# Fused attention and feed-forward on one core: unit loads, place and engine of the weight conversion's steps, one round more

## The chip, the core and the metric

The kernel runs on one core of a Trainium2 chip. The metric is the device time in microseconds of one execution; the median of three runs of the kernel before is 602.66 us (602.04 to 603.43). Engines are called by their names and, in the profile, by short ones: TensorE (PE; PEld is its weight load), VectorE (DVE), ScalarE (ACT), GpSimd (POOL), SyncE (SP, which here only issues transfers).

## What is computed

A decayed linear attention over blocks of 64 positions, then two feed-forward layers. The weights of the layers arrive as float64.

```python
def _attn_ref(q, k, v, lam):                 # B, H, S, D = 2, 8, 768, 64
    for b in range(S // 64):
        intra = (qb @ kb.T * Dmask) @ vb                 # Dmask = lam ** (i - j), i >= j
        inter = (qb * lam_pow) @ kv_state
        out[:, :, sl] = intra + inter
        kv_state = lam_block * kv_state + (kb * rev_pow).T @ vb
def _moe_ref(x, w_in, w_out):                # 1536 x 512, d_ff 2048
    h = x @ w_in
    g = where(h >= 1, h, where(h <= -1, 0, (h + 1) ** 2 / 4))
    return g @ w_out
def _moe2_ref(x, w_gate, w_val, w_out):      # d_ff 1536
    return (sigmoid(x @ w_gate) * (x @ w_val)) @ w_out
```

## The kernel before

**Attention.** It is cut into 16 units (batch, pair of heads, half of the sequence) and runs in 8 pairs of units, `for k in range(nu // 2)`; blocks of 128 positions are used. A unit's data is one array of 128 rows with four parts of 384 values: q, k, k by rows, v by rows. For each unit `scores` (L825) multiplies q and k on TensorE, `weigh` (L854) multiplies by the decay table `DT` on VectorE into `pT`, `values` (L886) multiplies with v; `pre_k` (L793, L800) scales k into `kd`, `updates` (L843) makes the state's increments, `states` (L869) scans them on VectorE, `pre_q` (L811) scales q on GpSimd into `qs`, `queries` (L905) adds the part from the state. `high` (L917, ScalarE) and `low` (L921, VectorE) split the result into `xh` and `xl`, two parts whose products stand for one product of higher precision.

**Loads.** `u_load` loads a unit through SP. Units 0 to 3 come in two transfers each (L694, rows of 3 KB), units 4 and 5 in four each (L686, rows of 1.5 KB), the later ones in one (L699, rows of 6 KB). In `tables` the first halves of units 0, 1 and 2 go first, then their second halves, units 3 and 4, then the tables `qp` and `DT`, which come through a DRAM buffer `pd` in rows of 512 bytes, then unit 5 and the others. `scores` of units 0, 1 and 2 stand ahead of the pairs.

**Conversion of the weights.** A piece is 128x512 float64 values, in the order `pieces`; pieces 0 to 3 are the first layer's input weights for its first four groups of columns n, 4 to 7 the output weights of the same groups. SP loads it into one of three `raw` tiles. Then *words* (`w_words`: two passes on ScalarE, L107 and L109, or three behind the attention, L107, L114, L115), *float* (`w_float`: L121 and L123 on VectorE, then an integer addition L125), *high* (`w_high`, L129 on ScalarE, the rounded half) and *low* (`w_low`, L133, the rest). Behind the attention a round (`w_round`) does one such step for each of three successive pieces, addition and rest on VectorE. In the attention the steps are jobs, W for words, F for float, H for high and low: the table `JOBS` gives for a pair a list for each of three places, and there the addition and the rest are on GpSimd. The places are: behind the scan, behind the weighing, and at the pair's end.

**Feed-forward in the attention's tail.** `feed_forward` is a generator whose steps are drawn by `next(steps)` in pairs 5 to 7. `hidden(n)` (L227, L228, L229) is 12 matmuls for group n and a block of 512 tokens: the high half of the piece first, the low half second. u0, u1, ... below are the entries of `seq`, u0 to u3 being n = 0 to 3 of the first tokens. Behind each, ScalarE (L259, L254) and VectorE (L263, *r*) make the activation, ScalarE (L246, *gh*) and VectorE (L247, *gl*) split it. `project` (L282) multiplies with the output weights (pieces 4 to 7) into four banks `a`; `flush` (L300, L302) copies them into `part`. In pair 5 hidden(0) is drawn, in pair 6 hidden(1) and hidden(2), in pair 7 hidden(3). When the attention is over, `finish` does a projection and a round. `forms_first` adds sums of `xh` and `xl` (*f*, L384) on VectorE between these.

On each engine instructions run in the order in which the program writes them (`tc.manual_schedule()`); between engines only the semaphores of shared tiles order them.

```python
if k - 1 in AFT: next(steps)     # behind states(k)
convert()                        # first place
...
for i in ahead: weigh(i)
convert()                        # second place
queries(a); queries(b); high(a); low(a)
...
if k in AFT: next(steps)
convert()                        # third place
```

Of the kernel before, what the change touches and what calls it, by code (L numbers as in the profile page):

```python
# [7 lines left out]
F32 = mybir.dt.float32  # L8
# [10 lines left out]
P = 128  # L19
NP = H // 2  # L20
CU = 3
UT = CU * P
NHALF = S // UT
TT = 512
# [5 lines left out]
CST = 4 + PADW + P  # L30
NS = 2 * CU - 1
FORE, AFT = (6, 7), (5, 6)
JOBS = {4: (("W0",), ("F0",), ()), 5: (("H0", "W1"), ("F1",), ("H1", "W2")),
        6: (("F2", "H2"), ("W3",), ("F3", "W4")), 7: (("H3", "F4"), ("W5", "H4"), ("F5", "W6"))}
NQD = 2
UB = 6
NEARLY, NWIDE = 6, 4
WARM = 2
NWP, NRAW = 10, 3

# [2 lines left out]
def fused_kernel(ctx: ExitStack, tc: tile.TileContext, qkv, qd, cst, w1, w2, out):  # L43
# [150 lines left out]
    def w_job(job):  # L194

        i = int(job[1:])
        if job[0] == "W":
            assert prog["round"] == i and prog["loaded"] > i
            prog["round"] += 1
            w_words(i)  # L200
            w_load()
        elif job[0] == "F":
            w_float(i, pool)
        else:
            w_high(i)
            w_low(i, pool)
            w_forms(i)
# [27 lines left out]
    seq = []  # L235
# [96 lines left out]
    def feed_forward():  # L332
        def finish():
            project(*behind.pop(0))
            if u is not seq[-1]:
                w_round()

        for u in seq:
            n, t, first, last = u
            h = hidden(n, t, 0)  # L340
            split()
            yield
            r = act1(h, n, t)
            act1_end(r, h)
            fresh.append((u, r))
            yield
            j = seq.index(u)
            while attention_over and len(behind) >= (4 if j < NEARLY else 3 if j < 8 else 2):
                finish()
        split()  # L350
# [312 lines left out]
    with ExitStack() as actx:  # L663
# [11 lines left out]
        raw_u = {}  # L675

        def u_load(i, js=range(2)):
# [1 line left out]
                return  # L679
            b, p, h = units[i]  # L680
            if NWIDE <= i < NEARLY:
                tag = ("gh", "gl")[i - NWIDE]
                raw_u[i] = [gp.tile([P, TT], F32, tag=tag, name=f"u{i}_{j}")[:, 0:UT]
                            for j in range(4)]
                for j in range(4):
                    sp.dma_start(out=raw_u[i][j], in_=qkv[b, p, h][:, j])  # L686
                return
            if i < NEARLY:

# [32 lines left out]
        def tables():  # L722
# [2 lines left out]
            dm = [tp.tile([P, 512], F32, tag="r", bufs=5, name=f"dm{j}")[:, 0:2 * (PADW + P)]  # L725
                  .rearrange("p (h x) -> p h x", h=2) for j in range(2)]
            sp.dma_start(out=cs[:, 0:CST], in_=cst)
            for j in range(2):
                for i in range(3):
                    u_load(i, (j,))  # L730
            for i in range(3, 5):
                u_load(i)
            dve.memset(zero, 0.0)
            for j in range(2):
# [51 lines left out]
        def pre_k(i):  # L786
# [1 line left out]
            b, p, h = units[i]  # L788
            kd[i] = sp2.tile([P, CU, 2, D], F32, tag="kd", name=f"kd{i}")
            for e in range(2):  # L790
                if i < 1 and not e or i // 2 - 1 in AFT and e:

                    pool.tensor_tensor(  # L793
                        out=kd[i][:, :, e],
                        in0=raw_u[i][2].rearrange("p (c h d) -> p c h d", c=CU, h=2)[:, :, e],
                        in1=DT[:, 2 * p + e, P - 1:P].unsqueeze(1).to_broadcast([P, CU, D]),
                        op=ALU.mult,
                    )
                    continue
# [124 lines left out]
        with tc.manual_schedule():  # L924
            tables()
            warm()
            for i in range(3):
                scores(i)
            pre_k(0)
            pre_k(1)  # L930
# [5 lines left out]
            for k in range(nu // 2):  # L936
                a, b = 2 * k, 2 * k + 1
                ahead = [i for i in (a + 2, b + 2) if i < nu]
                jobs = iter(JOBS.get(k, ((), (), ())))

                def convert():
                    for job in next(jobs):
                        w_job(job)

                if k:
# [14 lines left out]
                convert()  # L960
                for i in ahead:
                    pre_k(i)
                    if i != 2:
                        scores(i)
                if k == 0:
                    weigh(1)
                if k in FORE:
# [5 lines left out]
                queries(b)  # L973
                high(a)
                low(a)
                if ahead:
                    decay(k + 1)
                for i in ahead:
# [96 lines left out]
```

## Time and profile before

| | |
|---|---|
| median of three runs | 602.66 us |
| profiled execution, its own time | 602.4 us |
| its span | 600.6 us |
| TensorE busy | 582.8 us, 97% |
| VectorE busy | 439.8 us, 73% |
| ScalarE busy | 373.9 us, 62% |
| GpSimd busy | 86.9 us, 14% |
| granted clock, mean | 0.994 |

A profile is one execution. Spans and timelines count from its first instruction; its own time is 1.8 us longer than the span. Matmuls overlap in the pipeline, so a busy TensorE need not be at its peak: the distance from start to start tells the pace. The timeline gives behind an instruction the idle time of its engine ahead of it and what ended that time. Idle time on an engine that nothing waits for costs nothing. The page's 40 slices show loads at 291 to 375 GB/s in the first three slices (15 us each) and little later, and the granted clock at full in all slices but the fifth.

### The profile page before, as it was taken

What the parts mean: (1) busy time and instruction counts of PE and PEld (TensorE: products, weight loads), DVE (VectorE), ACT (ScalarE), POOL (GpSimd) and SP (SyncE); (2) the same over time, 40 slices, a digit from 0 to 9 for tenths busy, and PEclk for the clock granted to TensorE, in tenths of its full rate; (3) what the DMA queues carried; (4) which work ended last, traced back from release to release, by engine and by line L of the source; (5) the groups of instructions that cost most, each with busy time, mean ns of one, the idle gap of its engine ahead of it and who ended that gap; (6) DMA issues with size and microseconds to landing.
All of it is one profiled execution on the core that took longest, in us unless ns stands there. A gap on an engine that the chain in (4) does not pass through costs nothing.

```text
span 600.6 us, 8055 instructions
## 1 busy us (share of the span) xinstructions
PE 582.8 (97%) x3060; PEld 480.4 (80%) x3060; DVE 439.8 (73%) x717; ACT 373.9 (62%) x661; POOL 86.9 (14%) x92
## 2 busy tenths in 40 slices
PE   7898789999999999999999999999999999999997
PEld 5787568888888888888888887888888888888886
DVE  7685578879797978888788997694684685584444
ACT  6457576689686868676786687673583583451220
POOL 4446400000000000000000001231141151060000
PEclk9999799999999999999999999999999999999999
DMA  8991232012121221212131233131132031000013
GB/s 291 375 367 69 79 136 102 2 70 94 48 73 68 72 70 69 72 44 75 59 105 47 80 109 106 46 113 64 35 106 70 24 113 41 2 0 1 0 71 140
DMA packets 16678, 52.59 MB, mean 88 GB/s; under 512 B 1784, under 2 KB 4096, under 8 KB 16640
## 3 DMA queue, kind: packets, MB, share of 16 engines
q1 hardware_dynamic: 16624, 52.08, 25.3%
q8 instruction: 24, 0.39, 0.3%
q14 instruction: 14, 0.11, 0.1%
q10 hardware_dynamic: 16, 0.01, 0.0%
HBM read 48.92 MB, written 3.15 MB: 87 GB/s over the span
## 4 chain that ended last, share of the span: by engine, by line
PE 85%; DVE 5%; ACT 4%; DMA 3%; POOL 2%; issue 1%; SPq 0%; POOLq 0%; DVEq 0%; ACTq 0%
PE a L282 35%; PE p L418 25%; PE h L228 7%; PE h L229 7%; PE h L227 7%; DMA u<-in_qkv 3%; PE x L905 1%; PE x L886 1%; PE s L825 1%; DVE part L409 1%; POOL wr L125 1%; POOL w L133 1%; ACT xth L370 0%; ACT w L129 0%; DVE wr L125 0%
## 5 line engine op out<-in xcount | busy, mean ns | idle before, releaser
L282 PE MATMUL a<-gh,w 128*128 128x512 f32 x384 | 118.7, 390 | 2.0 <-DVE w L133 2.0
L304 DVE TENSOR_TENSOR part<-part,a 128x512 f32<-128x512 f32 x132 | 83.3, 680 | 12.4 <-PE a L282 12.4
L227 PE MATMUL h<-xh,w 128*128 128x512 f32 x224 | 88.3, 394 | 3.3 <-ACT w L129 3.3
L228 PE MATMUL h<-xh,w 128*128 128x512 f32 x224 | 88.5, 395 | 1.9 <-POOL w L133 1.9
L282 PE MATMUL a<-w,gh 128*128 128x512 f32 x288 | 88.7, 389 | 0.0
L229 PE MATMUL h<-xl,w 128*128 128x512 f32 x224 | 88.1, 393 | 0.0
L282 PEld LDWEIGHTS a<-gh,w 128*128 128x128 f32 x384 | 72.0, 188 | 17.6 <-DVE w L133 2.4
L282 PE MATMUL a<-gl,w 128*128 128x512 f32 x192 | 74.7, 389 | 0.0
L282 PEld LDWEIGHTS a<-w,gh 128*128 128x128 f32 x288 | 54.1, 188 | 11.2
L151 POOL TENSOR_TENSOR wr<-wr 128x256 f32<-128x256 f32 x16 | 13.2, 824 | 328.7 <-DVE w L133 328.1
L282 PE MATMUL a<-w,gl 128*128 128x512 f32 x144 | 56.0, 389 | 0.0
L129 ACT ACTIVATE w<-wr 128x512 fp32r<-128x512 f32 x68 | 42.4, 623 | 21.1 <-POOL wr L125 11.2
L227 PEld LDWEIGHTS h<-xh,w 128*128 128x128 f32 x224 | 42.5, 190 | 12.7 <-ACT w L129 3.6
L228 PEld LDWEIGHTS h<-xh,w 128*128 128x128 f32 x224 | 42.6, 190 | 11.4 <-POOL w L133 2.7
L229 PEld LDWEIGHTS h<-xl,w 128*128 128x128 f32 x224 | 42.6, 190 | 8.8
L133 DVE TENSOR_TENSOR w<-wr,w 128x512 fp32r<-128x512 f32 x63 | 47.0, 746 | 3.2 <-ACT w L129 3.2
L114 ACT ACTIVATE wc<-raw 128x512 uint16<-128x512 uint32 x61 | 47.9, 785 | 0.0
L107 ACT ACTIVATE wr<-raw 128x512 f32<-128x512 f32 x68 | 45.1, 663 | 4.2 <-POOL s L159 3.6
L115 ACT ACTIVATE wc<-raw 128x512 f16<-128x512 f32 x61 | 47.0, 770 | 0.0
L125 DVE CUSTOM_DVE_ANT_0 wr<-wr,wc 128x1024 uint16<-128x1024 uint16 x62 | 44.0, 709 | 3.0 <-ACT wc L115 0.2
L246 ACT ACTIVATE gh<-r 128x512 fp32r<-128x512 f32 x40 | 25.0, 625 | 30.4 <-DVE r L263 20.1
L282 PEld LDWEIGHTS a<-gl,w 128*128 128x128 f32 x192 | 36.0, 188 | 7.4
(117 smaller groups left out, 1048.2 us busy)
## 6 DMA issues: line engine op xcount, KB each, us to landing
raw<-in_w SPq DMA_DIRECT2D x68, 512.0 KB, 3.4
u<-in_qkv SPq DMA_DIRECT2D x10, 768.0 KB, 8.8
u<-in_qkv SPq DMA_DIRECT2D x8, 384.0 KB, 6.4
out<-part SPq DMA_DIRECT2D x12, 256.0 KB, 2.1
u<-in_qkv SPq DMA_DIRECT2D x8, 192.0 KB, 5.6
DT<-pd SPq DMA_DIRECT2D x1, 256.0 KB, 5.7
qp<-pd SPq DMA_DIRECT2D x2, 96.0 KB, 4.9
DT<-pd SPq DMA_DIRECT2D x1, 128.0 KB, 5.8
```

Source lines behind the costliest of these rows:

```text
L107: act.activation(r, hi.bitcast(F32), AF.Copy, scale=2.0 ** -112)
L114: act.activation(limb(U16)[:, :, 0], lo, AF.Copy, scale=2.0 ** -29)
L115: act.activation(limb(F16)[:, :, 1], hi.bitcast(F32), AF.Copy, scale=2.0 ** -60)
L125: eng.tensor_tensor(out=ri, in0=ri, in1=c, op=ALU.add)
L129: act.activation(ws[i][:, 0], tmps[i][0], AF.Copy)
L133: eng.tensor_tensor(out=ws[i][:, 1], in0=r, in1=ws[i][:, 0].bitcast(F32), op=ALU.subtract)
L227: pe.matmul(h, lhsT=wh, rhs=xh[:, k, tt], start=(k == 0), stop=False)
L228: pe.matmul(h, lhsT=wl, rhs=xh[:, k, tt], start=False, stop=False)
L229: pe.matmul(h, lhsT=wh, rhs=xl[:, k, tt], start=False, stop=(k == NP - 1))
L282: pe.matmul(accs[j], lhsT=a, rhs=b_, start=(first and m == 0), stop=(last and m == 2))
L304: dve.tensor_tensor(out=o, in0=o, in1=accs[j], op=ALU.add)
L418: pe.matmul(o, lhsT=a, rhs=b_, start=(start and k == 0 and m == 0), stop=(k == HK - 1 and m == 2), skip_group_check=True)
```

## The change

Loads: units 0 to 4 come in two transfers each, unit after unit; unit 5 comes in one, into the tile `part0`, which is first written much later by `flush`. `scores(2)` moves into the first pair, beside `scores(3)`. Conversion: F adds on VectorE and no longer on GpSimd; a pair has four places, the new third one behind `low(a)`; F0, H2, W3, F3, H3, F5 and others move by a place. All of `kd` but one half of unit 0's is scaled on ScalarE; before, four halves in pairs 5 and 6 were on GpSimd. `finish` does one round more for the fifth and sixth entry of `seq`.

```diff
@@ -30,11 +30,11 @@
 CST = 4 + PADW + P
 NS = 2 * CU - 1
 FORE, AFT = (6, 7), (5, 6)
-JOBS = {4: (("W0",), ("F0",), ()), 5: (("H0", "W1"), ("F1",), ("H1", "W2")),
-        6: (("F2", "H2"), ("W3",), ("F3", "W4")), 7: (("H3", "F4"), ("W5", "H4"), ("F5", "W6"))}
+JOBS = {4: ("W0", "", "F0", ""), 5: ("H0 W1", "F1", "", "H1 W2"),
+        6: ("F2", "H2 W3", "F3", "H3 W4"), 7: ("F4", "H4 W5", "F5", "W6")}
 NQD = 2
 UB = 6
-NEARLY, NWIDE = 6, 4
+NEARLY, NWIDE = 6, 5
 WARM = 2
 NWP, NRAW = 10, 3
 
@@ -200,7 +200,7 @@
             w_words(i)
             w_load()
         elif job[0] == "F":
-            w_float(i, pool)
+            w_float(i, dve)
         else:
             w_high(i)
             w_low(i, pool)
@@ -333,6 +333,8 @@
         def finish():
             project(*behind.pop(0))
             if u is not seq[-1]:
+                w_round()
+            if u in seq[4:6]:
                 w_round()
 
         for u in seq:
@@ -679,11 +681,10 @@
                 return
             b, p, h = units[i]
             if NWIDE <= i < NEARLY:
-                tag = ("gh", "gl")[i - NWIDE]
-                raw_u[i] = [gp.tile([P, TT], F32, tag=tag, name=f"u{i}_{j}")[:, 0:UT]
-                            for j in range(4)]
-                for j in range(4):
-                    sp.dma_start(out=raw_u[i][j], in_=qkv[b, p, h][:, j])
+                a = part[0].rearrange("p a b -> p (a b)")[:, 0:4 * UT].rearrange(
+                    "p (j t) -> p j t", j=4)
+                sp.dma_start(out=a, in_=qkv[b, p, h])
+                raw_u[i] = [a[:, j] for j in range(4)]
                 return
             if i < NEARLY:
 
@@ -725,10 +726,7 @@
             dm = [tp.tile([P, 512], F32, tag="r", bufs=5, name=f"dm{j}")[:, 0:2 * (PADW + P)]
                   .rearrange("p (h x) -> p h x", h=2) for j in range(2)]
             sp.dma_start(out=cs[:, 0:CST], in_=cst)
-            for j in range(2):
-                for i in range(3):
-                    u_load(i, (j,))
-            for i in range(3, 5):
+            for i in range(5):
                 u_load(i)
             dve.memset(zero, 0.0)
             for j in range(2):
@@ -788,7 +786,7 @@
             b, p, h = units[i]
             kd[i] = sp2.tile([P, CU, 2, D], F32, tag="kd", name=f"kd{i}")
             for e in range(2):
-                if i < 1 and not e or i // 2 - 1 in AFT and e:
+                if i < 1 and not e:
 
                     pool.tensor_tensor(
                         out=kd[i][:, :, e],
@@ -924,7 +922,7 @@
         with tc.manual_schedule():
             tables()
             warm()
-            for i in range(3):
+            for i in range(2):
                 scores(i)
             pre_k(0)
             pre_k(1)
@@ -936,10 +934,10 @@
             for k in range(nu // 2):
                 a, b = 2 * k, 2 * k + 1
                 ahead = [i for i in (a + 2, b + 2) if i < nu]
-                jobs = iter(JOBS.get(k, ((), (), ())))
+                jobs = iter(JOBS.get(k, ("",) * 4))
 
                 def convert():
-                    for job in next(jobs):
+                    for job in next(jobs).split():
                         w_job(job)
 
                 if k:
@@ -960,8 +958,7 @@
                 convert()
                 for i in ahead:
                     pre_k(i)
-                    if i != 2:
-                        scores(i)
+                    scores(i)
                 if k == 0:
                     weigh(1)
                 if k in FORE:
@@ -973,6 +970,7 @@
                 queries(b)
                 high(a)
                 low(a)
+                convert()
                 if ahead:
                     decay(k + 1)
                 for i in ahead:
```

What this does to the order on the engines is shown at three places. VectorE in pair 6 from the rest of unit 12 to the scan of pair 7, before (`wr` is the float tile of a piece, here piece 3, `r_0`, `gl_0` activations of u1 and `sc` the scan):

```order
L921 TENSOR_TENSOR xl<-x_734,xh 128x384
L263 SCALAR_TENSOR_TENSOR r_0_823<-r_0_823,h_0_0_776 128x512
L247 TENSOR_TENSOR gl_0_841<-r_0_823,gh_0_840 128x512
L121 TENSOR_SCALAR wr_799<-wr_799 128x512
L123 SCALAR_TENSOR_TENSOR wr_799<-raw_644,wr_799 128x512
L921 TENSOR_TENSOR xl<-x_809,xh 128x384
L869 SCALAR_TENSOR_TENSOR sc_97<-ld,uu_859 128x320
```

and now:

```order
L919 TENSOR_TENSOR xl<-x_723,xh 128x384
L121 TENSOR_SCALAR wr_788<-wr_788 128x512
L123 SCALAR_TENSOR_TENSOR wr_788<-raw_633,wr_788 128x512
L125 ISA wr_788<-wr_788,wc_789 128x1024
L263 SCALAR_TENSOR_TENSOR r_0_815<-r_0_815,h_0_0_762 128x512
L247 TENSOR_TENSOR gl_0_833<-r_0_815,gh_0_832 128x512
L919 TENSOR_TENSOR xl<-x_798,xh 128x384
L867 SCALAR_TENSOR_TENSOR sc_97<-ld,uu_851 128x320
```

The float step of piece 3 moved ahead of the activation of u1, and its addition (printed ISA, `wc` being the second word) stands behind it.

VectorE behind the attention, from the activation of u5, before (`w` in L133 is the low half of pieces 6 and 7, the `wr` ahead of it are pieces 7 and 8):

```order
L263 SCALAR_TENSOR_TENSOR r_1_1041<-r_1_1041,h_1_0_1024 128x512
L121 TENSOR_SCALAR wr_999<-wr_999 128x512
L125 ISA wr_999<-wr_999,wc_1000 128x1024
L133 TENSOR_TENSOR w_1059<-wr_936,w_1059 128x512
L247 TENSOR_TENSOR gl_1_1083<-r_1_1041,gh_1_1082 128x512
L384 TENSOR_TENSOR f_1086<-xh 128x1024
L263 SCALAR_TENSOR_TENSOR r_1_1088<-r_1_1088,h_1_0_1069 128x512
L384 TENSOR_TENSOR f_1086<-f_1086,xl 128x1024
L121 TENSOR_SCALAR wr_1061<-wr_1061 128x512
L125 ISA wr_1061<-wr_1061,wc_1062 128x1024
L133 TENSOR_TENSOR w_1107<-wr_999,w_1107 128x512
```

and now:

```order
L263 SCALAR_TENSOR_TENSOR r_1_1030<-r_1_1030,h_1_0_1013 128x512
L121 TENSOR_SCALAR wr_988<-wr_988 128x512
L125 ISA wr_988<-wr_988,wc_989 128x1024
L133 TENSOR_TENSOR w_1048<-wr_925,w_1048 128x512
L121 TENSOR_SCALAR wr_1050<-wr_1050 128x512
L125 ISA wr_1050<-wr_1050,wc_1051 128x1024
L133 TENSOR_TENSOR w_1060<-wr_988,w_1060 128x512
L247 TENSOR_TENSOR gl_1_1084<-r_1_1030,gh_1_1083 128x512
L386 TENSOR_TENSOR f_1087<-xh 128x1024
L263 SCALAR_TENSOR_TENSOR r_1_1089<-r_1_1089,h_1_0_1070 128x512
```

The round that makes the low half of piece 7 moved ahead of the split of u5, the sum `f` and the activation of u6.

SP at the start, before, from the first transfer of unit 4 (`u_0` to `u_3` are its parts, the second group of four is unit 5):

```order
L686 DMA u_0_121<-in_qkv 128x384
L686 DMA u_1_122<-in_qkv 128x384
L686 DMA u_2_123<-in_qkv 128x384
L686 DMA u_3_124<-in_qkv 128x384
L766 DMA qp<-pd 64x3x128 x2
L772 DMA DT<-pd 128x2x128
L772 DMA DT<-pd 128x4x128
L686 DMA u_0_177<-in_qkv 128x384
L686 DMA u_1_178<-in_qkv 128x384
L686 DMA u_2_179<-in_qkv 128x384
L686 DMA u_3_180<-in_qkv 128x384
L699 DMA u_185<-in_qkv 128x1536
```

and now:

```order
L695 DMA u_0_121<-in_qkv 128x768
L695 DMA u_1_122<-in_qkv 128x768
L764 DMA qp<-pd 64x3x128 x2
L770 DMA DT<-pd 128x2x128
L770 DMA DT<-pd 128x4x128
L686 DMA part_79<-in_qkv 128x1536
L700 DMA u_174<-in_qkv 128x1536
```

Unit 4 has two transfers, unit 5 one, both at the same place relative to the tables.

## Rows read from the trace of the kernel before

**Rows 1.** Waits of TensorE, whole span: us in total, times, longest.

```profile
PE h L227 <- ACT w L129: 3.3, 1, 3.3
PE a L282 <- DVE w L133: 2.0, 1, 2.0
PE h L228 <- POOL w L133: 1.9, 2, 1.4
```

**Rows 2.** Timeline of TensorE: start us, busy us, engine, line, operation, count, [idle before].

```profile
40.24 1.78 PE L905 MATMUL x<-qs,sc 64*64 64x128 f32 x20
...
48.62 0.50 PE L227 MATMUL h<-xh,w 128*128 128x512 f32 x1
...
51.57 1.41 PE L905 MATMUL x<-qs,sc 64*64 64x128 f32 x20
...
52.91 0.49 PE L227 MATMUL h<-xh,w 128*128 128x512 f32 x1
...
56.60 0.88 PE L886 MATMUL x<-pT,u 128*64 128x128 f32 x12
...
57.89 0.83 PE L886 MATMUL x<-pT,u 128*64 128x128 f32 x12
...
62.03 0.52 PE L227 MATMUL h<-xh,w 128*128 128x512 f32 x1 [3.31 <-ACT w L129]
...
68.91 1.45 PE L905 MATMUL x<-qs,sc 64*64 64x128 f32 x20
```

**Rows 3.** Busy us (instructions) of each engine by stretch, granted clock, DMA share, GB/s.

```profile
24.00:42.00 18.00, 17.89 (x309) 16.20 (x307) 14.98 (x29) 11.46 (x28) 7.19 (x7) 1.00 0.98 373
...
58.00:72.00 14.00, 9.32 (x63) 6.80 (x59) 7.19 (x11) 7.97 (x16) 6.05 (x4) 0.76 0.22 77
...
92.00:112.00 20.00, 20.00 (x90) 16.56 (x89) 17.25 (x25) 12.18 (x21) 0.00 (x0) 1.00 0.16 52
```

**Rows 4.** Timeline of ScalarE, VectorE and GpSimd around piece 3.

```profile
53.59 0.65 ACT L107 ACTIVATE wr<-raw 128x512 f32<-128x512 f32 x1
...
54.33 1.94 DVE L854 TENSOR_TENSOR pT<-s,DT 128x384 f32<-128x384 f32 x4
...
56.19 0.55 DVE L921 TENSOR_TENSOR xl<-x,xh 128x384 fp32r<-128x384 f32 x1
...
58.75 0.42 DVE L121 TENSOR_SCALAR wr<-wr 128x512 uint32<-128x512 uint32 x1
...
59.20 0.69 DVE L123 SCALAR_TENSOR_TENSOR wr<-raw,wr 128x512 uint32<-128x512 uint32 x1
...
60.04 1.27 POOL L125 TENSOR_TENSOR wr<-wr,wc 128x512 int32<-128x512 int32 x1 [2.84 <-DVE wr L123]
...
61.34 0.63 ACT L129 ACTIVATE w<-wr 128x512 fp32r<-128x512 f32 x1 [0.47 <-POOL wr L125]
...
62.05 1.81 POOL L133 TENSOR_TENSOR w<-wr,w 128x512 fp32r<-128x512 f32 x1 [0.74 <-ACT w L129]
...
62.65 1.76 DVE L247 TENSOR_TENSOR gl<-r,gh 128x512 fp32r<-128x512 f32 x1
```

**Rows 5.** Groups, VectorE then GpSimd: shapes, count, busy us, mean ns, idle before.

```profile
L125 DVE CUSTOM_DVE_ANT_0 wr<-wr,wc 128x1024 uint16<-128x1024 uint16 x62 | 44.0, 709 | 3.0 <-ACT wc L115 0.2
...
L125 POOL TENSOR_TENSOR wr<-wr,wc 128x512 int32<-128x512 int32 x6 | 8.1, 1356 | 19.4 <-DVE wr L123 11.2 <-PE uu L843 8.2
```

**Rows 6.** Timeline of the three engines that wait for unit 5.

```profile
19.02 1.00 POOL L811 TENSOR_TENSOR qs<-u,qp 128x384 f32<-128x384 f32 x1 [1.77 <-DMA u<-in_qkv]
...
19.49 0.94 PE L825 MATMUL s<-u,u 64*128 64x128 f32 x12 [2.48 <-DMA u<-in_qkv]
...
19.95 0.80 ACT L800 ACTIVATE kd<-u,DT 128x192 f32<-128x192 f32 x2 [1.42 <-DMA u<-in_qkv]
```

**Rows 7.** Two stretches of the loads, columns as in rows 3.

```profile
13.00:16.00 3.00, 3.00 (x64) 2.77 (x60) 2.74 (x7) 1.45 (x4) 0.27 (x1) 1.00 1.10 247
...
19.00:24.00 5.00, 4.51 (x80) 4.13 (x82) 2.43 (x5) 2.79 (x7) 2.00 (x2) 1.00 1.01 395
```

## Prediction

> **What bounds the kernel now.** I read the waits of TensorE first, then its timeline around the longest, then the engines that end them. TensorE is the bound nearly everywhere: from 92 to 112 us its busy time fills the stretch [rows 3], and the table of waits names none of 1 us or more behind that, so time can only come out of the first 92 us. There the table of waits [rows 1] names three: 3.3 us for the high half of a weight piece (ScalarE, L129), 1.9 us for low halves (GpSimd, L133), 2.0 us for a low half that VectorE makes in a later round. The reader is to see that the first two are one story. A `hidden` product is 12 matmuls: hidden(1) runs from 48.62 to 51.57, 2.95 us. hidden(2) begins at 52.91 and lasts until 56.60; hidden(3) should follow values(14), which ends at 57.89 + 0.83 = 58.72, begins at 62.03, and lasts until 68.91 [rows 2]. Part of that last length is the clock: the granted clock averages 0.76 over 58 to 72 us [rows 3], because it stood at half, the 1.2 GHz level, for part of it after TensorE had been idle.
>
> Why is piece 3 late? Its words start on ScalarE at 53.59, but its float step starts on VectorE only at 58.75; GpSimd adds from 60.04 for 1.27 us, ScalarE rounds at 61.34, GpSimd subtracts from 62.05 to 63.86 [rows 4]. Four engine changes, one behind the other, and in front of them VectorE's own queue.
>
> **What the edits remove.** Terms, as far as they stand on TensorE's path:
> - hidden(2) longer than hidden(1): 3.69 - 2.95 = 0.74 us.
> - idle before hidden(3): 62.03 - 58.72 = 3.31 us.
> - hidden(3) longer: 6.88 - 2.95 = 3.93 us, the wait for the low half and the halved clock together. The second goes if the idle goes.
> - the later wait of a projection (L282) for VectorE's low half: 2.0 us [rows 1].
> - queries(10) and (11) take 1.78 us against 1.41 later [rows 2]: their scaled queries stand behind the addition of piece 0 on GpSimd. That addition leaves GpSimd: 0.37 us.
> Together 10.35 us.
>
> **Do they go?** The addition on VectorE is the operation that already stands at L125, 0.71 us against 1.36 us on GpSimd [rows 5]: six of them put 4.3 us on VectorE and take 8.1 us from GpSimd. VectorE was busy 7.19 of the 14 us from 58 to 72 [rows 3], so there is room, but its order matters, since everything on it runs in sequence. So I lay the new order out with the durations of the rows: a pass of ScalarE over 128x512 0.63 to 0.65 us, VectorE's steps 0.42 and 0.69 us, four weighings 1.94 us, a rest `xl` 0.55 us [rows 4], the new addition 0.71 us [rows 5]. Times are on the clock of before, with the loads of the start left aside; all are estimates.
> Pair 6: VectorE ends the scan at 47.4 and r of u0 at 48.1, the float step of piece 2 at 49.9; ScalarE rounds it by 50.6, GpSimd subtracts by 51.9. hidden(2), which now follows at 52.6, finds both halves. So 0.74 goes.
> Float step of piece 3: it now stands straight behind `xl` of unit 12 and ahead of r of u1. Weighing ends at 52.4, `xl` at 52.95, the three float operations at 54.7; r of u1 at 55.35, its gh at 56.0, then ScalarE rounds piece 3 by 56.6, GpSimd subtracts by 57.9. hidden(2) ends at 55.6, values(13), the updates and values(14) take 2.1 us, so hidden(3) asks for the high half at 57.7 and the low half at 58.0. It just fits, with 0.1 us to spare; each us of slip is a us lost. 3.31 and 3.93 go, and with an idle this short so does the half clock.
> Piece 4: its float step stands behind r of u2, which needs two ScalarE passes behind `xh` of unit 13. That ends r at 60.25, the float step at 62.0, rounding at 62.7, GpSimd at 64.05. The first projection asks for the low half at 63.15. A **new wait of 0.9 us**, where before there was none. Bounds: 0 if each of these steps runs 0.1 us quicker, 2.5 us if GpSimd and VectorE block one another as at 62.65, where a step of 0.69 us took 1.76 us beside GpSimd's subtraction [rows 4]. I take 0.9, since only the end of gl of u2 touches that subtraction in my layout.
> Pieces 5 and 6 are ready 0.9 and 0.6 us ahead of their projections. Piece 7, whose wait was the 2.0 us, is made one round sooner: its low half comes at 78.5 and is asked for at 80.2. So that wait goes, though VectorE has less time. The first partial sums must leave their banks by 87.6 for the projection of u4; VectorE copies the last at 86.5.
> The round that is added is taken from later, not new work. Its words wait for raw weights: SP loads a raw tile when the float step or the words have freed it, so each load moves with its round, and the words follow it by 3 us or more; if a load fell behind, ScalarE's queue with gh and r would stand behind it.
> Four scalings of `kd` go from GpSimd to ScalarE, some 0.4 us each, 1.8 us in all. They lie between the words and gh and are in the layout (kd of units 14 and 15 until 48.85, gh of u0 behind them); without that cover they would delay gh of u0 by 0.8 us, which the projection needs 13 us later.
>
> **The loads at the start.** This part goes the other way. Unit 5 came in four pieces, and scores(5) started at 19.49 on the first two; GpSimd used the first at 19.02, ScalarE the third at 19.95 [rows 6]. So pieces land 0.47 us apart and the fourth at about 20.4 (estimate). Now it is one transfer, and scores(5) waits for all of it. If nothing is faster, that is 0.9 us later. From below: the stretch 13 to 16 us moved 247 GB/s where 19 to 24 moved 395 [rows 7]; if large rows closed all of that dip, the unit would land 3 x (1 - 247/395) = 1.1 us sooner, at 19.3 less some 0.2 for fewer transfers, 0.4 us earlier than scores(5) began. I take 0.7 us later: the pieces already follow at 0.47 us for 196 KB, 418 GB/s, so little is to be won by size, and the small rows of the tables stand ahead of unit 5 in the queue as before. The delay passes on in full, as TensorE is busy in every pair behind it, 17.89 of 18 us from 24 to 42 [rows 3]. scores(2) moves from idle time behind the first scores into the path, 0.9 us; the wait of 2.48 us before scores(5) hides it [rows 6]. If unit 5 came at 17.5, it would cost that 0.9. Unit 5 lies in `part0`, first written by the copies after 90 us, and piece 0 takes the tile of unit 0, long read: no wait from either.
> The Trainium skill's page DMA: Bandwidth & Descriptors (Bandwidth) says to batch transfers to 1 MiB and more, with 64 KB far from peak. By that, four transfers joined into one would be a clear gain, the end at -0.4 us; the 0.47 us between landings here does not bear it out.
>
> **Sum.** The profiled execution took 602.4 us (span 600.6), 0.26 under the median of 602.66. 602.4 - 10.35 + 0.9 + 0.7 = 593.65, say **593.6 us**. Its own range: 602.4 - 10.35 - 0.4 = 591.6 to 602.4 - 10.35 + 2.5 + 0.9 = 595.4.
>
> **Rivals.**
> 1. VectorE becomes the bound between 45 and 92 us. It gets 4.3 us more there, and one round of 1.8 us sooner, in a stretch that is to be some 9 us shorter; my margins are 0.1, 0.6, 0.9 and 1.1 us. For it: from 92 to 112 VectorE was already busy 17.25 of 20 us [rows 3]. Against it: that saturation caused no wait. If three of the four turn into waits of 1 us, 593.65 + 3 = 596.7; range 595.4 to 599. GpSimd's five subtractions stay and can hold VectorE, 1.07 us a time by the row at 62.65 [rows 4]. The Trainium skill's page SBUF — State Buffer (Who interferes with whom) says that a VectorE instruction with two SBUF inputs and GpSimd's reads lock one another out for a whole instruction; the row at 62.65 agrees.
> 2. The half clock comes back at the start. TensorE idled 2.48 us before scores(5) and the clock stayed at 1.00 [rows 6, 7]; 3.31 us and more before hidden(3) ended at half. Now it is 2.9 us, between them. The price is what it cost in hidden(3): from the low half's end at 63.86 to 68.91 it took 5.05 us where 11 of 12 matmuls of hidden(1) take 2.70, so 2.35 us: 596.0.
> 3. The added round does nothing where it stands (no tile free, or the raw words late), and the 2.0 us stay: 595.7.
> 4. The loads do close the dip and no wait for piece 4 appears: 591.2 to 591.6.
> 5. Slower than before: the float step now stands on VectorE ahead of the second `xl` and of the scan that the queries of the next pair need. If it is held there, because ScalarE's words are late, VectorE stands still with scan and weighings queued behind it, and TensorE runs dry in pairs 5, 6 and 7. Each such wait costs what hidden(3) cost, 3.31 + 3.93 = 7.2 us. One is not enough; from the second on the loss, 14.5 us, passes the 10.35 us gained: 602.4 - 8.75 + 14.5 = 608. In my layout words 0 to 3 end 1 to 3 us before their float steps, so this is unlikely.
>
> **Chances.** Forecast 0.62; rival 1 0.19; rival 2 0.05; rival 3 0.05; rival 4 0.04; rival 5 0.05. The range 591.3 to 597.6 holds the forecast, rivals 2 and 3, most of 4 and somewhat over half of rival 1: about 0.85 by these, 0.8 with what I have not thought of. A measurement of this kernel tells 0.2%, 1.2 us, from no change. Faster by more than that 0.95, within it 0.01 (a rival 5 of one and a half waits), slower 0.04.
>
> **What would show it.** Right: no wait of TensorE over 1 us from 24 to 92 us but the one for unit 5; hidden(1), (2) and (3) alike at about 3 us; clock 1.00 throughout; a short wait for GpSimd's low half before the first projection; no wait at the projection of piece 7; scores(5) at about 20.2. Wrong: waits on L133 or on `a` banks in several places (rival 1), a granted clock of 0.5 near 20 us (rival 2), a wait on VectorE's L133 as before (rival 3), scores(5) before 19.5 (rival 4), waits on the scan (rival 5).

## The result, and the profile after

The changed kernel takes 596.8 us (median; 595.83 to 597.33) where the kernel before takes 603.04 us beside it: ratio 0.9891, 95% interval 0.9863 to 0.992. It is faster, as forecast, and lies inside the range, but 3.2 us above the forecast of 593.6. The two profiled executions are 602.4 and 596.35 us, 6.05 us apart; the forecast's steps added up to 8.75. In the listing of the changed kernel most lines of the attention stand two numbers lower (L823 is the old L825, L903 the old L905).

Waits of TensorE after, whole span (us in total, times, longest), to be held against [rows 1]:

```profile
PE s L823 <- DMA part<-in_qkv: 2.9, 1, 2.9
...
PE h L228 <- POOL w L133: 0.9, 1, 0.9
...
PE a L282 <- POOL w L133: 0.6, 1, 0.6
...
PE h L227 <- ACT w L129: 0.4, 1, 0.4
```

The 3.3 us for a high half have become 0.4, the 2.0 us for VectorE's low half are gone, a wait of 0.6 us at a projection is new. The longest is now that for unit 5, which lies in `part`.

TensorE's timeline after (start us, busy us, line, operation, [idle before]), the places of [rows 2] and [rows 6]:

```profile
20.09 0.94 PE L823 MATMUL s<-part 64*128 64x128 f32 x12 [2.89 <-DMA part<-in_qkv]
20.96 2.36 PE L903 MATMUL x<-qs,sc 64*64 64x128 f32 x20
...
25.92 1.61 PE L823 MATMUL s<-u 64*128 64x128 f32 x24
...
42.27 1.41 PE L903 MATMUL x<-qs,sc 64*64 64x128 f32 x20
...
50.14 0.50 PE L227 MATMUL h<-xh,w 128*128 128x512 f32 x1
...
57.44 0.88 PE L884 MATMUL x<-pT,u 128*64 128x128 f32 x12
...
59.91 0.50 PE L227 MATMUL h<-xh,w 128*128 128x512 f32 x1 [0.36 <-ACT w L129]
...
61.27 0.50 PE L228 MATMUL h<-xh,w 128*128 128x512 f32 x1 [0.86 <-POOL w L133]
...
63.99 1.41 PE L903 MATMUL x<-qs,sc 64*64 64x128 f32 x20
...
67.24 0.50 PE L282 MATMUL a<-gh,w 128*128 128x512 f32 x1 [0.62 <-POOL w L133]
...
69.87 0.39 PE L227 MATMUL h<-xh,w 128*128 128x512 f32 x1
...
86.19 0.39 PE L227 MATMUL h<-xh,w 128*128 128x512 f32 x1
```

The last two are the starts of hidden for u4 and u7. Before, these and scores(6) stood here:

```profile
23.74 1.73 PE L825 MATMUL s<-u 64*128 64x128 f32 x24
...
73.94 0.39 PE L227 MATMUL h<-xh,w 128*128 128x512 f32 x1
...
92.62 0.39 PE L227 MATMUL h<-xh,w 128*128 128x512 f32 x1
```

Stretches after (busy us and instructions of TensorE, its weight loads, VectorE, ScalarE, GpSimd; granted clock, DMA share, GB/s); the last two are those of [rows 3], the second starts 0.6 us later than there:

```profile
21.20:24.60 3.40, 3.40 (x34) 3.07 (x34) 1.42 (x3) 0.80 (x2) 1.76 (x2) 0.50 1.01 423
24.60:42.00 17.40, 17.40 (x321) 15.99 (x320) 13.90 (x26) 10.65 (x26) 4.53 (x6) 1.00 0.92 353
58.00:72.00 14.00, 12.17 (x104) 9.47 (x101) 10.17 (x19) 11.25 (x21) 2.56 (x2) 1.00 0.30 113
92.00:112.00 20.00, 20.00 (x90) 16.56 (x89) 17.06 (x21) 9.23 (x15) 0.00 (x0) 1.00 0.01 4
```

The clock has moved: around hidden(3) it is now 1.00, where it averaged 0.76; behind scores(5) it is 0.50, the 1.2 GHz level, where it was 1.00.

ScalarE, VectorE and GpSimd around piece 3 after, against [rows 4]:

```profile
54.62 2.18 POOL L809 TENSOR_TENSOR qs<-u,qp 128x384 f32<-128x384 f32 x2
...
55.96 1.39 DVE L123 SCALAR_TENSOR_TENSOR wr<-raw,wr 128x512 uint32<-128x512 uint32 x1
...
57.38 0.69 DVE L125 CUSTOM_DVE_ANT_0 wr<-wr,wc 128x1024 uint16<-128x1024 uint16 x1
...
59.24 0.61 ACT L129 ACTIVATE w<-wr 128x512 fp32r<-128x512 f32 x1
...
59.94 1.28 POOL L133 TENSOR_TENSOR w<-wr,w 128x512 fp32r<-128x512 f32 x1 [3.13 <-ACT w L129]
```

The rounding of piece 3 starts at 59.24 where it was 61.34, though the whole program came 2.18 us later out of the loads. But the float step at 55.96 takes 1.39 us, twice its 0.69, while GpSimd scales queries.

The starts of the same work, subtracted, tell where the time went. "Gained" is the change from the line above:

| work on TensorE | before | after | after - before | gained | forecast |
|---|---|---|---|---|---|
| scores(5) starts | 19.49 | 20.09 | +0.60 | -0.60 | -0.7 |
| scores(6) | 23.74 | 25.92 | +2.18 | **-1.58** | 0 |
| queries(10) | 40.24 | 42.27 | +2.03 | 0.15 | 0 |
| hidden(1) | 48.62 | 50.14 | +1.52 | 0.51 | 0.37 |
| values behind hidden(2) | 56.60 | 57.44 | +0.84 | 0.68 | 0.74 |
| hidden(3) starts | 62.03 | 59.91 | -2.12 | 2.96 | 3.31 |
| queries(14) | 68.91 | 63.99 | -4.92 | **2.80** | 3.93 |
| hidden of u4 | 73.94 | 69.87 | -4.07 | -0.85 | -0.9 |
| hidden of u7 | 92.62 | 86.19 | -6.43 | 2.36 | 2.0 |
| end, own time | 602.4 | 596.35 | -6.05 | -0.38 | 0 |
| sum | | | | 6.05 | 8.75 |

From u7 on the two traces run in step; the last matmul still starts 6.43 us sooner (590.15 for 596.58), and the 0.38 us are behind it.

### The profile page after: what moved, and what is told of

Read it like the earlier page. It is cut to its first block, busy times and chain, and to the rows that moved or that the text cites. A ratio compares the mean times of both kernels' runs of the same rounds, so it can differ in the third digit from the quotient of the medians.

```text
span 594.5 us, 8055 instructions
## 1 busy us (share of the span) xinstructions
PE 583.1 (98%) x3060; PEld 481.8 (81%) x3060; DVE 442.6 (74%) x723; ACT 374.8 (63%) x665; POOL 76.1 (13%) x82
## 3 DMA queue, kind: packets, MB, share of 16 engines
HBM read 48.92 MB, written 3.15 MB: 88 GB/s over the span
## 4 chain that ended last, share of the span: by engine, by line
PE 84%; DVE 7%; ACT 4%; DMA 2%; issue 1%; SPq 0%; POOL 0%; DVEq 0%; ACTq 0%
PE a L282 36%; PE p L420 25%; PE h L227 7%; PE h L228 7%; PE h L229 7%; DMA part<-in_qkv 1%; DVE wr L125 1%; DMA pd<-pw 1%; PE x L884 1%; PE x L903 1%; PE s L823 1%; DVE wr L123 1%; DVE pT L852 1%; DVE part L411 1%; ACT w L129 1%
## 5 line engine op out<-in xcount | busy, mean ns | idle before, releaser
L228 PE MATMUL h<-xh,w 128*128 128x512 f32 x224 | 87.4, 390 | 0.9 <-POOL w L133 0.9
L227 PE MATMUL h<-xh,w 128*128 128x512 f32 x224 | 87.6, 391 | 0.4 <-ACT w L129 0.4
L125 DVE CUSTOM_DVE_ANT_0 wr<-wr,wc 128x1024 uint16<-128x1024 uint16 x68 | 48.1, 708 | 3.4 <-ACT wc L115 0.2
L133 DVE TENSOR_TENSOR w<-wr,w 128x512 fp32r<-128x512 f32 x63 | 47.1, 747 | 3.2 <-ACT w L129 3.2
```

The lines of the kernel that those rows point to most:

```text
L125: eng.tensor_tensor(out=ri, in0=ri, in1=c, op=ALU.add)
L133: eng.tensor_tensor(out=ws[i][:, 1], in0=r, in1=ws[i][:, 0].bitcast(F32), op=ALU.subtract)
L227: pe.matmul(h, lhsT=wh, rhs=xh[:, k, tt], start=(k == 0), stop=False)
L228: pe.matmul(h, lhsT=wl, rhs=xh[:, k, tt], start=False, stop=False)
```

## The experiments

**Theory.** The 2.7 us between forecast and profile are two things: the clock falls to half behind the longer wait for unit 5 (1.58), and two GpSimd scalings of queries hold float steps of VectorE, which leaves the waits at hidden(3) (1.48 = 0.35 + 1.13). **Rivals:** VectorE is simply too full; or the loads are no worse than before and the loss is elsewhere. Unless a line says otherwise, each kernel is the changed one with the edit shown. Each ratio is to the kernel before, run in the same series (its medians: 602.77 to 603.24 us).

| kernel | median, us (range) | ratio to before (95%) |
|---|---|---|
| changed kernel | 596.8 (595.83 to 597.33) | 0.9891 (0.9863 to 0.992) |
| changed kernel again | 596.77 (596.56 to 596.93) | 0.9896 (0.9872 to 0.9919) |
| unit 5 in two transfers | 594.3 (593.46 to 594.75) | 0.9848 (0.982 to 0.9877) |
| loads of before | 595.24 (593.22 to 596.69) | 0.9865 (0.984 to 0.989) |
| scores(4) thrice | 595.64 (594.23 to 598.31) | 0.9877 (0.9838 to 0.9917) |
| scalings of units 12 to 15 earlier | 595.68 (594.23 to 596.88) | 0.9872 (0.984 to 0.9903) |
| without the added round | 599.21 (596.45 to 601.38) | 0.9938 (0.9908 to 0.9969) |
| before, with the added round | 600.67 (599.35 to 601.91) | 0.995 (0.9932 to 0.9967) |
| addition on GpSimd | 598.9 (597.61 to 599.19) | 0.9934 (0.9909 to 0.9958) |
| old places | 600.08 (598.17 to 601.58) | 0.9947 (0.9927 to 0.9967) |
| halves, scalings of 14 and 15 earlier | 594.42 (592.53 to 594.92) | 0.986 (0.9816 to 0.9903) |
| the same, two low halves on VectorE | 593.25 (592.25 to 593.84) | 0.9836 (0.9798 to 0.9874) |
| the same, scores(4) twice | 592.44 (591.99 to 592.98) | 0.9824 (0.9804 to 0.9845) |

### The load of unit 5

**In two transfers.**

```diff
-                sp.dma_start(out=a, in_=qkv[b, p, h])
+                for j in (0, 2):
+                    sp.dma_start(out=a[:, j:j + 2], in_=qkv[b, p, h][:, j:j + 2])
```

> Against the changed kernel (596.8 us median, 596.35 in its profiled execution), unit 5 alone is loaded otherwise: two transfers into the same tile, q and k first. Theory: the shortfall at the start is two things, scores(5) 0.6 us later than before (20.09 against 19.49) because it waits for the whole unit, and a granted clock of 0.5 from 21.16 to 24.57 that follows the idle time of 2.89 us and costs 1.58 us. With halves scores(5) starts at about 19.5, the idle is about 2.3 us, the clock stays at 1.00: 2.2 us less, 594.6 us. Rival: the clock falls whatever the idle is here; then only 0.6 us is gained, 596.2 us.

Measured 594.3, near the theory's time. Its timeline at scores(5) and the queries behind, then the stretch in which its clock was at half:

```profile
19.44 0.94 PE L824 MATMUL s<-part 64*128 64x128 f32 x12 [1.37 <-DMA part<-in_qkv]
20.31 0.50 PE L904 MATMUL x<-qs,sc 64*64 64x128 f32 x4
...
9.40:12.70 3.30, 3.30 (x38) 2.91 (x36) 1.90 (x4) 1.80 (x6) 3.20 (x4) 0.50 1.03 414
```

The clock is at full behind scores(5). It was at half earlier instead, from 9.3 to 12.7 us, so it did not stay at full as the theory had it; that cost nothing, since TensorE then waited less for unit 5 (1.37 us). The waits at hidden(3) were as in the changed kernel. That the two transfers land sooner is borne out by the other profiles: in the four kernels with two transfers scores(5) began between 18.56 and 19.44 us, in the seven with one between 19.21 and 20.36.

**Loads of before.** All loads, and the place of scores(2), as in the kernel before; conversion, `kd` and rounds as changed. The lines that load unit 5, which are again those of before in the diff of the change, are left out here.

```diff
-            for i in range(5):
+            for j in range(2):
+                for i in range(3):
+                    u_load(i, (j,))
+            for i in range(3, 5):
                 u_load(i)
...
-            for i in range(2):
+            for i in range(3):
                 scores(i)
```

> The changed kernel with all loads as before: unit 5 in four transfers, first halves of units 0 to 2 first, scores(2) ahead of the pairs. Theory (the new loads cost 0.6 us and, with the longer wait, often the half clock, 1.6 us): scores(5) at 19.5, median 594.5 to 595.5, 1.3 to 2.3 under the changed kernel of this series. Rival (the loads of after are no worse, the half clock comes as often with those of before): the same time as the changed kernel.

**The changed kernel again**, no edit.

> The changed kernel once more, with more executions. Theory (its time varies by where the load of unit 5 lands and by whether the clock falls to half behind that wait; a stretch at half is 3.41 us long and costs 1.6 us): 595 with none, 596.5 with one, 598 with two; the mean granted clock of an execution, 1.00, 0.997, 0.994, goes down as its time goes up, and scores(5) lies between 19.2 and 20.3. Rival (the variation is elsewhere, in VectorE's chains): no order between clock and time.

These two ran side by side: 595.24 and 596.77 us. By the medians the new loads lose some 1.5 us, as the theory had it, though the intervals overlap a little. A single profile would not have told it:

```profile
19.98 0.96 PE L827 MATMUL s<-u,u 64*128 64x128 f32 x10 [2.88 <-DMA u<-in_qkv]
```

is the one with the old loads and

```profile
20.36 0.49 PE L823 MATMUL s<-part 64*128 64x128 f32 x4 [3.47 <-DMA part<-in_qkv]
```

the changed kernel again; in both the clock fell behind it, to half. With the old loads three of five executions had a mean granted clock of 0.999 or 1.00 (593.22, 593.75, 595.24 us) and two less (0.997 with 595.83, 0.994 with 596.69); of the changed kernel none of eight had over 0.997. The order of clock and time that was expected is nearly there with the old loads, but not within the changed kernel: 596.56 to 596.84 at 0.997, 596.93 at 0.993. That part was a miss.

**Less idle time before scores(5).** The sums are formed three times into the same banks, the second and third time repeating the first.

```diff
-                    scores(i)
+                    scores(i, 3 if i == 4 else 1)
...
-            for c in range(CU):
+            for c in list(range(CU)) * times:
```

> The changed kernel with the twelve matmuls of scores(4) done three times over, so that TensorE is busy for 1.8 us of the 2.89 us in which it waits for unit 5; the load is as in the change. Theory (the clock falls because of the idle): scores(5) still starts at 20.1, the clock stays at 1.00, queries(2) and (3) take 1.4 us and not 2.36: 1.6 us less, 595.2 us. Rival (the slow stretch from 21 to 24.6 us comes from the loads, or the clock falls anyway): 596.8 us and queries of 2.3 us.

595.64, but from 594.23 to 598.31, an interval that holds the changed kernel too. In the profile the clock stayed at 1.00, but there unit 5 also landed early (scores(5) at 19.43), so this run alone decides nothing.

### The queries' scalings beside VectorE

```diff
+                for i in ahead if k >= 5 else ():
+                    pre_q(i)
                 if k - 1 in AFT:
                     next(steps)
                 convert()
...
-                for i in ahead:
+                for i in ahead if k < 5 else ():
                     pre_q(i)
```

> The changed kernel with the scalings of q for units 12 to 15 on GpSimd one place sooner, ahead of the low halves of pieces 0 and 2. Theory: the waits of hidden(3), 0.36 and 0.86 us, come from VectorE's float step of piece 3, whose second operation took 1.39 us in place of 0.69 us beside a scaling on GpSimd (that took 2.18 us for two in place of 2.0); away from the scalings both float operations take 0.69 us, hidden(3) waits 0.3 us in all at most, gain 0.9 us, 595.9 us. Rival (VectorE has simply too much to do ahead of piece 3): both waits stay within 0.2 us, 596.8 us.

595.68, near the theory's 595.9; but its executions lie between 594.23 and 596.88 us, so the time alone decides nothing, and the rows have to. VectorE and GpSimd of this kernel at pair 5, TensorE's wait there, then the float step of piece 3:

```profile
39.25 1.15 POOL L809 TENSOR_TENSOR qs<-u,qp 128x384 f32<-128x384 f32 x1 [1.79 <-DMA u<-in_qkv]
39.58 1.37 DVE L123 SCALAR_TENSOR_TENSOR wr<-raw,wr 128x512 uint32<-128x512 uint32 x1
...
43.02 1.25 PE L903 MATMUL x<-qs,sc 64*64 64x128 f32 x17 [0.67 <-DVE sc L867]
...
56.06 0.69 DVE L123 SCALAR_TENSOR_TENSOR wr<-raw,wr 128x512 uint32<-128x512 uint32 x1
```

The float step of piece 3 is back at 0.69 us, and both waits at hidden(3) are gone from the table of waits. But the scaling now meets the float step of piece 0, which takes 1.37; the scan behind it on VectorE is late, and queries(10) wait 0.67 us. The collision is the cause: where it goes, the slow step goes with it.

### The added round

```diff
-            if u in seq[4:6]:
-                w_round()
```

> The changed kernel without the added round. Theory: the wait of TensorE for VectorE's low half of piece 7 comes back, 2.0 us by the row of the kernel before, perhaps 0.5 us more or less: 598.8 us. Rival: with the earlier pieces done sooner the round is in time anyway, 596.8 us.

599.21, the time of the theory; the wait of [rows 1] is back, at the first matmul that takes piece 7's low half:

```profile
83.53 0.50 PE L282 MATMUL a<-gh,w 128*128 128x512 f32 x1 [2.09 <-DVE w L133]
```

**The round alone**, in the kernel before:

> The kernel before with nothing but the added round behind the fifth and sixth entry of seq. Theory (the round is worth its wait by itself): the wait of 2.0 us at the projection with piece 7 goes, no other comes; 2.0 to 2.4 under before. Rival (it pays only where VectorE has the addition out of the way, or pulls the loads of raw weights into a wait elsewhere): within 0.5 us of before.

600.67 against 602.97 beside it, 2.3 us less: by the medians the round is worth about the same with and without the rest. Here is scores(5) of this kernel and the clock behind:

```profile
19.34 1.65 PE L827 MATMUL s<-u,u 64*128 64x128 f32 x12 [2.37 <-DMA u<-in_qkv]
...
18.90:25.70 6.80, 6.36 (x66) 5.83 (x68) 1.91 (x4) 2.25 (x6) 2.94 (x3) 0.50 1.01 413
```

With the loads of before and a shorter wait than the 2.48 us of [rows 6], the clock fell here, still within the wait, and for 6.8 us.

### Engine of the addition, and places of the steps

```diff
-            w_float(i, dve)
+            w_float(i, pool)
```

> The addition of F goes back to GpSimd, all else as after (596.8 us). Theory (the engine of the addition is part of the gain): queries(10), (11) take 1.78 us again (+0.4), the chain of piece 3 is longer by an addition of 1.36 for 0.7 us and the two qs scalings, 2.2 us, stand between GpSimd's addition and its subtraction, so hidden(3) waits 1 to 2.5 us more for its low half; piece 4 +0.6: 599 to 600. Rival (VectorE has become the bound, and its 4.3 us more are where the missing 2.7 us went): about 595.5, faster than after.

598.9, 2.1 above the changed kernel; the rival's 595.5 is out. GpSimd and TensorE at piece 3:

```profile
58.17 1.29 POOL L125 TENSOR_TENSOR wr<-wr,wc 128x512 int32<-128x512 int32 x1 [1.93 <-DVE wr L123]
59.41 2.45 POOL L809 TENSOR_TENSOR qs<-u,qp 128x384 f32<-128x384 f32 x2
61.82 1.26 POOL L133 TENSOR_TENSOR w<-wr,w 128x512 fp32r<-128x512 f32 x1
...
63.14 0.50 PE L228 MATMUL h<-xh,w 128*128 128x512 f32 x1 [1.58 <-POOL w L133]
```

The scalings stand between addition and subtraction, as expected. So what VectorE is spared is lost in GpSimd's queue. The clock has a part in it: in this profile it fell a second time, from 64.1 to 67.5 us, behind that wait of 1.58 us, and hidden(3) took 6.25 us where it took 4.08 in the changed kernel.

**Old places**, addition on VectorE:

```diff
-JOBS = {4: ("W0", "", "F0", ""), 5: ("H0 W1", "F1", "", "H1 W2"),
-        6: ("F2", "H2 W3", "F3", "H3 W4"), 7: ("F4", "H4 W5", "F5", "W6")}
+JOBS = {4: ("W0", "F0", "", ""), 5: ("H0 W1", "F1", "", "H1 W2"),
+        6: ("F2 H2", "W3", "", "F3 W4"), 7: ("H3 F4", "W5 H4", "", "F5 W6")}
```

> The jobs at the places of before (F2 H2 together, F3 W4 at the end of pair 6, H3 F4 in pair 7), addition on VectorE. Theory (places and engine both are needed): the float step of piece 3 stands behind r and gl of u1 again and gains only the quicker addition; hidden(3) waits 1.5 us more for the high half, 1 us more for the low, and the clock goes to half, 2.35 us: 601. Rival (the engine alone does it): 596.5 to 597.5.

600.08, the side of the theory. Its float step of piece 3, its hidden(3) and the clock there:

```profile
59.06 0.69 DVE L123 SCALAR_TENSOR_TENSOR wr<-raw,wr 128x512 uint32<-128x512 uint32 x1
...
61.27 0.49 PE L227 MATMUL h<-xh,w 128*128 128x512 f32 x1 [3.37 <-ACT w L129]
...
62.80:66.20 3.40, 3.40 (x9) 2.62 (x10) 2.04 (x4) 1.90 (x4) 1.15 (x1) 0.50 0.44 161
```

The story of [rows 2] and [rows 4] is back, half clock and all. Neither engine nor place does it alone. The scaling of `kd` on ScalarE was in all these kernels but the one with the round alone; what it is worth by itself was not measured.

### Putting the repairs together

Unit 5 in two transfers, and only the scalings of units 14 and 15 earlier (`k == 6` for `k >= 5`, `k != 6` for `k < 5` in the edit above):

> Unit 5 in two transfers, and GpSimd's qs of units 14 and 15 alone one place earlier. Theory (what is missing is the load with its half clock, and VectorE's float step held by the scalings beside hidden(3)): both go, the two gaps before and in hidden(3) shrink from 2.0 to 0.5 us, no wait of queries(10) as it was with the scalings of units 12 and 13 moved too: 594.3 - 1.4 = 592.9, as the forecast without the price of the load, 592.9. Rival (a saved wait comes back later, since VectorE is the bound behind it): 594.

The profiled execution took 592.53 us, at a mean clock of 1.00, close to the forecast without the price of the load, and its waits at hidden(3) are down to 0.4 us with none new later. But the median is 594.42, the rival's value, with the other three (594.14 to 594.92) at 0.997. In the median it can't be told from the two transfers alone; where the clock fell in the three was not recorded.

**Two low halves on VectorE** in addition:

```diff
-            w_low(i, pool)
+            w_low(i, dve if i in (3, 4) else pool)
```

> As the kernel with halves and early scalings, and the low halves of pieces 3 and 4 also on VectorE (0.69 for GpSimd's 1.28 us). Theory: the gap of 0.5 in hidden(3) and that of 1.1 us at the first projection lose 0.5 to 0.6 us each: 591.9. Rival (VectorE is full there; what it gets delays gl of u1 and u2 and the scan): same as the kernel without it or up to 1 us slower, 592.9 to 594.

593.25: 1.2 under the kernel without it, which ran beside it, as the theory's difference of 1.0; its absolute value lies in the rival's range, as that kernel's did. VectorE did take the two steps without a loss. The intervals overlap, so that it gains is not shown by these times alone. **And scores(4) twice:**

```diff
-                    scores(i)
+                    scores(i, 2 if i == 4 else 1)
```

> Unit 5 in two transfers, scalings of units 14 and 15 one place earlier, low halves of pieces 3 and 4 on VectorE, and scores(4) done twice into the same banks (the second time repeats the first), so that TensorE idles 0.9 us less before unit 5. Theory: no gap left over 1.3 us but the one for unit 5, which stays under 2 us; median 592.3, and no execution at a mean clock under 0.997. Rival (the half clock in these kernels comes from the idle times before 10 us, which nothing here touches): 593.2, as without the repetition.

592.44 (591.99 to 592.98), the theory's value. Its rows at scores(5) and the first projection:

```profile
18.65 0.94 PE L824 MATMUL s<-part 64*128 64x128 f32 x12 [0.94 <-DMA part<-in_qkv]
...
62.13 0.49 PE L282 MATMUL a<-gh,w 128*128 128x512 f32 x1 [0.25 <-ACT w L129]
...
62.85 0.50 PE L282 MATMUL a<-gh,w 128*128 128x512 f32 x1 [0.23 <-DVE w L133]
```

The wait of 0.9 for hidden(3)'s low half is gone from its table of waits, that of 0.6 at the projection is down to two of a quarter. This kernel beats both: 10.8 us under before and 4.3 under the changed kernel, which ran in the same series (596.77). How much of the last 0.8 is the repeated scores is not separated, since the two ran in different series and their intervals overlap.

## Why the prediction was right or wrong

**What bounded the kernel** was read rightly: every microsecond gained lies ahead of u7, and behind it nothing was gained. The prediction's own range for its mechanism, 591.6 to 595.4, does not hold the 596.8 us; the wide one does, because it makes room for rivals 1 and 2, and a part of each came.

**hidden(2), queries(10) and the added round** came as summed: 0.68 for 0.74, 0.51 for 0.37, 2.36 for 2.0; the round was worth 2.4 us taken out and 2.3 put in alone. **The new wait for piece 4** was worked out at 0.9 and cost 0.85.

**hidden(3)** was mis-sized by 1.48 us: 0.35 of the idle before it and 1.13 of its length stayed. The step that failed is the layout of VectorE. It was to end the rounding of piece 3 at 56.6 and the subtraction at 57.9 on the clock of before, 58.1 and 59.4 with the 1.52 us by which the program was late at hidden(1); they ended at 59.85 and 61.22, some 1.8 us later. Two float steps, at 44.33 (piece 1) and at 55.96 (piece 3), took 1.39 us each for the 0.69 laid out: 1.4 of the 1.8. The layout asked only where GpSimd's *subtractions* touch VectorE. Its *scalings* now run beside the float steps. Nothing on GpSimd holds them back any more: at the new places an addition would stand ahead of them, as in the run that has it there, where they began at 59.41; and the scalings of `kd`, which came just ahead of them before, are on ScalarE now. These are GpSimd's rows in pair 6 before:

```profile
53.78 1.46 POOL L793 TENSOR_TENSOR kd<-u,DT 128x192 f32<-128x192 f32 x2
55.20 1.99 POOL L811 TENSOR_TENSOR qs<-u,qp 128x384 f32<-128x384 f32 x2
```

There the float step came 2 us behind the scalings, at 59.20 [rows 4]; now its earlier place brings it to 55.96, and the scalings start at 54.62. The collision at 44.33 reaches piece 3 through ScalarE, which waits for the late addition, rounds piece 1, makes the next words and only then the `xh` that VectorE stands still for:

```profile
46.65 0.63 ACT L129 ACTIVATE w<-wr 128x512 fp32r<-128x512 f32 x1 [1.78 <-DVE wr L125]
...
48.84 0.56 DVE L919 TENSOR_TENSOR xl<-x,xh 128x384 fp32r<-128x384 f32 x1 [1.82 <-ACT xh L915]
```

The prediction had quoted the rule that decides it, the Trainium skill's page SBUF — State Buffer (Who interferes with whom): a VectorE instruction with two SBUF inputs and GpSimd's reads exclude one another. The run with the scalings earlier agrees, 1.39 to 0.69 us at piece 3 and 0.69 to 1.37 at piece 0. So a part of rival 1's mechanism came, though not its premise: VectorE was not too full, since taking the additions off it cost 2.1 us, and giving it two low halves more cost nothing.

**The load** cost the 0.6 us that were forecast as 0.7. That larger rows win little was right; two transfers took 2.5 us less than one in the medians (the intervals just overlap). The Trainium skill's page DMA: Bandwidth & Descriptors (Bandwidth) asks for large transfers; no run here agrees that joining these gains.

**The half clock at the start**, rival 2, is what the chances missed: 0.05 for something that stood in six of the eight profiled executions, of all kernels here, in which scores(5) waited 2.37 us or more, and at scores(5) in none of the six with 2.02 or less. The forecast had put the wait of 2.9 between 2.48 (full) and 3.31 (half) and taken full. Its 2.9 is not what its own terms give: 2.48 + 0.7 for the load - 0.9 for scores(2) is 2.3 us. That 2.89 was measured is luck: with scores(2) in the path TensorE came to this wait only 0.2 us later than before (17.20 for 17.01), not 0.9. Its price was mis-sized the other way: 1.58 us, not 2.35, because the earlier half stretch had been twice as long (6.8 us against 3.4). That stretch in the kernel before:

```profile
62.40:69.20 6.80, 5.43 (x16) 3.77 (x17) 2.01 (x2) 1.84 (x4) 4.43 (x3) 0.50 0.26 97
```

**Together:** 593.65 + 1.58 (clock) + 1.48 (hidden(3)) + 0.06 (hidden(2)) + 0.38 (end) = 597.15, less 0.80 that went better than forecast (load 0.10, ahead of queries(10) 0.15, queries(10) and (11) 0.14, piece 4 0.05, the round 0.36) = 596.35, the profiled time.

**Rivals 3, 4 and 5** are out: the round did its work, scores(5) came later and not earlier, and no wait on the scan appeared except where an experiment put the scaling there.

## What to carry to other kernels

Taking work from one engine changes when the rest of its queue runs: before moving it, lay out not only the engine that receives it but also what the relieved engine will do in its place, and against which instruction of a neighbour that runs. When TensorE waits as long for a load as in those eight profiles (2.37 us and more), count the half clock there as likely, and hand over the load in the parts that its first reader needs. Judge a change of some microseconds by medians of a series with the old kernel in it, since the place where one load lands moves a single profile by as much.

## What the runs showed of the hardware

**Idle time alone does not decide the clock.** It fell at a wait of 2.37 us (before with the added round, above), behind one of 1.58 us (the addition on GpSimd, at hidden(3)), and stayed at full behind 3.15 us in the kernel with the old places; its scores(5) and the stretch behind it:

```profile
20.00 0.83 PE L823 MATMUL s<-part 64*128 64x128 f32 x10 [3.15 <-DMA part<-in_qkv]
...
21.00:24.60 3.60, 3.60 (x70) 3.31 (x72) 2.47 (x5) 2.27 (x7) 1.84 (x3) 1.00 1.01 423
```

What else decides it is left open.

**The same load lands at different times.** With one and the same sequence of transfers scores(5) began between 19.21 us (without the added round) and 20.36 us (changed kernel again), 1.15 us apart.

**A scaling on GpSimd doubles a step of VectorE beside it, but not every step.** In the changed kernel's pair 5, VectorE and GpSimd:

```profile
42.04 1.93 DVE L852 TENSOR_TENSOR pT<-s,DT 128x384 f32<-128x384 f32 x4
42.96 2.21 POOL L809 TENSOR_TENSOR qs<-u,qp 128x384 f32<-128x384 f32 x2
...
44.33 1.39 DVE L123 SCALAR_TENSOR_TENSOR wr<-raw,wr 128x512 uint32<-128x512 uint32 x1
```

Four weighings, one of whose inputs is a bank of TensorE's sums, keep the 1.94 us of [rows 4] beside the first scaling; the float step, with both inputs in SBUF, takes twice its time beside the second.
